# Moved load requests, an ACT copy, and re-timed weight splits and decode steps in a fused attention, MoE and gated-MLP kernel

## The chip, the cores and the metric

One Trainium2 chip, of which the kernel uses one core. The metric is the device time of one execution in microseconds (us), the median of several; lower is better.

## What is computed

The reference, cut to its three stages:

```python
# attention over pooled keys: q,k,v (8, 8, 576, 64); k and v are averaged over 8 neighbours -> 72
scores = q @ k_p.T / sqrt(64)
x = softmax(scores) @ v_p                  # -> x: 4608 tokens x 512
# MoE, top-1 of 8 experts
e = argmax(x @ w_gate); g = softmax(x @ w_gate)[e]
y = g * (relu(x @ w1[e]) @ w2[e])          # w1 (8, 512, 1024), w2 (8, 1024, 512)
# gated MLP, float64 weights
yn = y / sqrt(mean(y*y) + 1e-6) * rms_g
out = (silu(yn @ wg) * (yn @ wv)) @ w_out  # 512 -> 1536 -> 512
```

## The kernel before, in words

The program is one function, `fused`, written out in the order in which each engine gets its work. Float32 matmuls of the MoE and MLP are made of three fp32r ones: every operand is split into a rounded part `h` (a cast on ACT) and a rest `l` (a subtraction).

**Attention** (about 0 to 235 us) goes over 36 token tiles, n = 0 to 35 (loop at the end of the function's first half). A tile has an `emit_pt` (TensorE (PE) transposes of the probabilities), `emit_exp`, `emit_qt` for tile n+3, `emit_sc` (scores) for n+2, `emit_av` for n and `store` of the rows into `x_d` in DRAM. Between these lie five places "a" to "e"; `plan(n, place, f)` hangs a step on one, `run` issues what hangs there. So places are only positions in each engine's program: nothing runs before its operands are there, and an engine works its own list strictly in order. Nine tiles make two batches; the last of nine (tile 8, 17, 26, 35) is mixed and needs a zeroed block `qz` (L365, memset on POOL).

**Loads.** Ahead of the loop the requests for batches 0 and 1 are written out by hand for the SP queue (L763 to L779): `load_k`, `load_q(b, g, j)` (heads' half g, tokens' half j), `load_rows` (v) and `load_ends` (the last 64 key rows of several batches, eight requests of 48 KB). `sum_ends` on POOL adds those, `end_k` puts them into `kbd`, which the scores of that batch read. Requests share eight completion counters in turn, so a request is not issued before the one eight places ahead of it has landed.

**Routing.** `route_steps` gives for a group of tiles r1 (DVE: which expert), r3 (PE and DVE: rank inside the expert) and r4 (POOL: indirect stores of the token number to `ord_d`). After tile 18 `choose` to `choose_5` pick the expert for the first slots from what is known by then; `choose_2` writes the expert's number for SP (`first_expert`) and the places for `first_tokens`; `first_rows` gathers the rows of slot 0 into `xg` (L673), copies its logits to `lg0` (L676), and `xpose(0, c)` (in tiles 32 and 33) turns them on PE.

**First expert weights.** `load_w(i)` (tiles 25 to 28) brings eight blocks of 512 KB into `st`; `split_w(i, half)` makes `h` on ACT (L147, reported at the helper's line) and `l` on POOL (L148). Blocks 0 to 3 are w1, 4 to 7 w2.

**MoE slots** (about 235 to 700 us). `body(s)` works 256 tokens of one expert: eight `stage1(s, f)` (12 matmuls into one of four PSUM tiles `p`; relu `hh` on ACT, rest `hl` on DVE, which frees the tile), then `xpose` of the next slot, then `stage2` for one or two halves of 128 tokens. If the next slot has another expert ("fresh"), `change` and `change_half` split its weights beside this: w2 behind f = 3, the first half of w1 behind f = 4, the second behind f = 7, casts on ACT and four subtractions each on DVE.

**Decode steps.** In the same slots, `unit_steps(s, j)` turns float64 MLP weights into `uh` and `ul`, in two halves j = 0, 1 of five steps: s1 a square on ACT (writes `ub`), s2 two DVE instructions (write `ua`), s3 two (read `ub`, write `uh` and `ua`), s4 two (write `ub`), s5 one (reads `ub` and `ua`, writes `ul`). `ua` and `ub` are single buffers. Each step hangs on a place of `body`: 0 to 7 behind `stage1` f, 8 behind the next slot's `xpose` and w1 split, 9 behind the first half of `stage2`, 10 behind the second. `unit_load` brings the float64 data.

**MLP** (about 700 us to the end) has no part in the change.

Of the kernel before, what the change touches and what calls it, by code (L numbers as in the profile page):

```python
# [22 lines left out]
DM = 512  # L23
# [10 lines left out]
XW = DM + E  # L34
CUT = 18
SECOND = 30
EB = ((0,), (1, 2, 3), (4, 5, 6, 7))
# [12 lines left out]

R3 = [13, 17]

CW = [19, 30, 36, 46, 35, 52]

PLAIN = (0, 1, 2, 3, 4, 5)

# [25 lines left out]
def fused(ctx: ExitStack, tc: tile.TileContext, q, k, v, moe_w_gate, moe_w1, moe_w2,  # L82
          w_gate, w_val, w_out, rms_g, cst, out):
    nc = tc.nc
# [37 lines left out]
    lg0 = const.tile([128, 2, E], F32, name="lg0")  # L122
# [47 lines left out]
    def split_w(i, half, fresh=False):  # L170
        if fresh:
            for w, nm in ((w1h, "w1h"), (w1l, "w1l")) if i < 4 else ((w2h, "w2h"), (w2l, "w2l")):
                w[i % 4] = wtile(F32R, f"{nm}{i % 4}")
        hi, lo = (w1h[i], w1l[i]) if i < 4 else (w2h[i - 4], w2l[i - 4])
        c = slice(512 * half, 512 * half + 512)
        split(hi[:, c], lo[:, c], st[i][:, c], nc.gpsimd)
# [26 lines left out]
    def load_k(b):  # L203
        t = kq.setdefault(("k", b), [])
        for h4 in range(2):
            x = wtile(F32, f"k{h4}")
            nc.sync.dma_start(
                out=x.rearrange("p (h n) -> p h n", h=4),
                in_=k[b, 4 * h4:4 * h4 + 4, 0:512, :].rearrange("h (p r) d -> p h (r d)", r=4),
            )  # L210
            t.append(x)

    def load_q(b, g, j=None):
        t = kq["q", b] if ("q", b) in kq else kq.setdefault(("q", b), {})
        if g not in t:
            t[g] = wtile(F32, f"q{g}")
        c = slice(0, 256) if j is None else slice(128 * j, 128 * j + 128)
        nc.sync.dma_start(
            out=t[g].rearrange("p (h n) -> p h n", h=4)[:, :, c],
            in_=q[b, 4 * g:4 * g + 4, 0:512, :].rearrange("h (p r) d -> p h (r d)", r=4)[:, :, c])  # L220
# [10 lines left out]
    def load_ends(bs, eng=None):  # L231

        x = wtile(F32, "ke")
        n = len(bs)
        for h in range(H):
            (eng or nc.sync).dma_start(
                out=x[16 * h:16 * h + 16, 0:256 * n].rearrange("p (b n) -> p b n", b=n),
                in_=k[bs[0]:bs[-1] + 1, h, 512:576, :].rearrange("b (p r) d -> p b (r d)", r=4))
        kq["ke", bs] = x
# [26 lines left out]
    def load_rows(src, b, nm, hs=(0, 1, 2, 3)):  # L266
        t = kq.setdefault((nm, b), [])
        for h in hs:
            x = wtile(F32, f"{nm}{h}")
            nc.sync.dma_start(  # L270
                out=x[0:NP].rearrange("p (h n) -> p h n", h=2),
                in_=src[b, 2 * h:2 * h + 2].rearrange("h (p r) d -> p h (r d)", r=8))
            t.append(x)
# [321 lines left out]
    def xpose(s, c):  # L595

        px_ = px(c)
        for d in range(2):
            for z in range(2):
                nc.tensor.transpose(px_[:, d, 128 * z:128 * z + 128],  # L600
                                    xg[s][:, z, (2 * c + d) * 128:(2 * c + d) * 128 + 128], ident)
        hi, lo = (x[:, 2 * c:2 * c + 2] for x in xts[s])
        nc.scalar.copy(out=hi, in_=px_)
        nc.vector.tensor_tensor(out=lo, in0=px_, in1=hi, op=ALU.subtract)
        if c and s:
            gate_of(s)


    ev, xg, first = {}, {}, {}
# [60 lines left out]
    def first_rows():  # L670
        xg[0] = x_p.tile([128, 2, XW], F32, tag="xg0", bufs=1, name="xg0")
        for z in range(2):
            nc.gpsimd.indirect_dma_start(  # L673
                out=xg[0][:, z], out_offset=None, in_=x_d[0:CUT * 128, :],
                in_offset=bass.IndirectOffsetOnAxis(ap=tok0[:, z:z + 1], axis=0))
        nc.gpsimd.tensor_copy(out=lg0, in_=xg[0][:, :, DM:XW])  # L676
        xts[0] = tuple(wtile(F32R, "xt0").rearrange("p (c t) -> p c t", c=4) for _ in range(2))

    def second_tokens():
# [16 lines left out]
    def plan(n, where, f):  # L696
        at.setdefault((n, where), []).append(f)
# [42 lines left out]
        plan(CUT + i // 5, "abcde"[i % 5], f)  # L740
    for i in range(8):
        plan(CUT + 7 + i // 2, "ac"[i % 2], lambda i=i: load_w(i, ev[0], True))
        plan(CUT + 9 + (i + 1) // 2, "ca"[i % 2], lambda i=i: split_w(i, 0, True))
        plan(CUT + 9 + (i + 1) // 2, "eb"[i % 2], lambda i=i: split_w(i, 1))
    plan(CUT + 4, "e", choose_2)
    plan(CUT + 7, "e", choose_3)
    plan(CUT + 8, "e", choose_4)
    plan(CUT + 9, "e", choose_5)
    plan(SECOND - 2, "a", second_tokens)
    plan(SECOND, "c", second_rows)  # L750
    plan(NTL - 4, "b", lambda: xpose(0, 1))
# [19 lines left out]
    nc.sync.dma_start(out=wgl, in_=moe_w_gate.rearrange("(k p) e -> p k e", p=128))  # L771
    load_q(0, 1, 0)
    load_q(0, 0, 1)
    load_k(1)
    load_q(0, 1, 1)
    load_ends(EB[1])
    load_q(1, 0)
    load_rows(v, 1, "v")
    load_q(1, 1)  # L779
    nc.vector.memset(wg, 0.0)  # L780
    for t in vau:
# [171 lines left out]
    def unit_load(u, j):  # L953
        src, kk = unit_src(u, j)
        t = us_p.tile([128, 2 * DM + 2], I32 if wide else F32, tag="us", name="us")[:, 0:1024 if wide else 512]
        nc.sync.dma_start(out=t.rearrange("p (k n) -> p k n", k=kk), in_=src)
        ust[u, j] = t
# [41 lines left out]
    def unit_store(u):  # L999
        if stored(u):  # L1000
            for i, x in enumerate(held.pop(u)):
                nc.sync.dma_start(out=scr[u - EARLY, i], in_=x.bitcast(F32))
# [195 lines left out]
    late = []  # L1198
    for s in range(SURE):
        fill = {}  # L1200

        def put_in(place, f):
            fill.setdefault(place, []).append(f)

        if s == 0:
            for place, fs in tail.items():
                for f in fs:
                    put_in(place, f)
        if s == 1:
            put_in(0, lambda: gather(2))  # L1210
            put_in((1, 2), lambda: xpose(2, 0))
            put_in((1, 3), lambda: xpose(2, 1))
        for place, f in late:
            put_in(place, f)
        a = unit_steps(s, 0)
        b_ = unit_steps(s, 1)
        for place, f in zip((1, 2, 3, 5, 6) if s else [(0, 4)] * 5, a):
            put_in(place, f)
        if s + 1 < NU:
            put_in(7 if s else (0, 6), lambda s=s: unit_load(s + 1, 0))  # L1220
        else:
            put_in(7, ready)
            put_in(9, norm_0)
        for place, f in zip((7, 8, 8, 9) if s else [10] * 4, b_):
            put_in(place, f)
        late = [(0, b_[4]), (2, lambda s=s: unit_store(s))]
        if s + 1 < NU:
            late.append((1, lambda s=s: unit_load(s + 1, 1)))
        body(s, fill, 0 if s else 3)
        if s == 0:  # L1230
            sctx.close()
            vctx.close()
            psm = mctx.enter_context(tc.tile_pool(name="ps_m", bufs=1, space=PSUM))
            p1[:] = [psm.tile([128, T], F32, name=f"p1_{i}") for i in range(4)]
# [187 lines left out]
```

## Time and profile before

| | |
|---|---|
| median of 3 runs | 1651.44 us (1649.84 to 1652.1) |
| the profiled execution | 1655.93 us, of it span 1654.1 us |
| PE busy | 97% of the span, 9397 matmuls |
| DVE, ACT, POOL busy | 51%, 30%, 16% |
| granted TensorE clock, mean | 0.986 |
| DMA | 161.95 MB, mean 98 GB/s |

The span is cut into stages by what runs in them. For each the view of waits tells which engine was late, the timeline tells with what, and the granted clock tells the rest: 1.00 is 2.4 GHz, 0.50 is 1.2 GHz. Engine names: PE TensorE, DVE VectorE, ACT ScalarE, POOL GpSimd, SP the queue that issues DMAs. A line number is that of the kernel before; a helper's line stands for all its callers.

### The profile page before, as it was taken

To read this page: it belongs to the slowest core of one execution; us is meant where nothing else is said; L and a number is where in the kernel's file an instruction comes from. 1 tells how busy PE (TensorE), PEld (TensorE's weight loads), DVE (VectorE), ACT (ScalarE), POOL (GpSimd) and SP (SyncE) were. 2 spreads that over 40 slices of the span, in tenths; PEclk is the share of its full clock that TensorE was granted. 3 is DMA by queue.
4 is the path that set the end of the run, shared out by engine and by line. 5 is a ranking of instruction groups with operands and counts; after the bars stand their busy time and mean duration, and the time that the engine had idled before them with its cause. 6 is when DMAs were issued, how large, how long until landed. Compare 5 with 4: busy or idle time off the path is not lost. (4 is left out here: it accounts for less than half of the span.)

```text
span 1654.1 us, 26653 instructions
## 1 busy us (share of the span) xinstructions
PE 1596.7 (97%) x9397; PEld 1379.4 (83%) x9399; DVE 841.8 (51%) x1805; ACT 497.9 (30%) x1027; POOL 264.1 (16%) x363
## 2 busy tenths in 40 slices
PE   8999979989999989999999999999999999999997
PEld 6898868878888888998888888888888888888886
DVE  5688866688767686324443433333443333443222
ACT  3455623454434353322212112121221212122121
POOL 4687471110111011103000000000000000000000
PEclk9899989999999999999999999999999999999999
DMA  8977736476746463217400100010010001000000
GB/s 223 252 179 167 194 80 210 135 260 211 252 143 232 145 236 111 66 47 270 108 14 20 33 13 26 13 39 14 13 36 16 27 13 32 20 0 26 0 26 13
DMA packets 123515, 161.95 MB, mean 98 GB/s; under 512 B 36560, under 2 KB 85072, under 8 KB 123360
## 3 DMA queue, kind: packets, MB, share of 16 engines
q1 hardware_dynamic: 111328, 124.00, 26.4%
q0 software_dynamic: 11776, 35.91, 7.0%
q8 instruction: 77, 1.26, 0.3%
q14 instruction: 78, 0.64, 0.1%
q10 hardware_dynamic: 256, 0.13, 0.0%
HBM read 116.93 MB, written 43.08 MB: 97 GB/s over the span
## 5 line engine op out<-in xcount | busy, mean ns | idle before, releaser
L1319 DVE SCALAR_TENSOR_TENSOR th<-th,g 128x512 f32<-128x512 f32 (+1 forms) x120 | 76.1, 634 | 470.2 <-ACT th L1318 470.2
L1316 PE MATMUL g<-xh,rl 128*128 128x512 f32 (+1 forms) x576 | 217.5, 378 | 0.0
L1315 PE MATMUL g<-xl,rh 128*128 128x512 f32 (+1 forms) x576 | 217.5, 378 | 0.0
L1314 PE MATMUL g<-xh,rh 128*128 128x512 f32 (+1 forms) x576 | 217.5, 378 | 0.0
L1318 ACT ACTIVATE th<-g 128x512 f32<-128x512 f32 (+1 forms) x120 | 66.6, 555 | 461.8 <-PE g L1316 461.8
L1345 POOL DMA_INDIRECT out_dram<-o,tk x36 | 34.6, 962 | 815.7 <-ACT o L1344 788.6
L1340 PE MATMUL po<-rl,a 128*128 128x512 f32 x360 | 140.5, 390 | 1.5 <-DMA rl<-scr 1.5
L1339 PE MATMUL po<-rh,a 128*128 128x512 f32 x360 | 140.3, 390 | 0.0
L1341 PE MATMUL po<-rh,a 128*128 128x512 f32 x360 | 140.2, 389 | 0.0
L1315 PEld LDWEIGHTS g<-xl,rh 128*128 128x128 f32 x576 | 108.4, 188 | 20.2
L1314 PEld LDWEIGHTS g<-xh,rh 128*128 128x128 f32 x576 | 108.4, 188 | 20.2
L1316 PEld LDWEIGHTS g<-xh,rl 128*128 128x128 f32 x576 | 108.4, 188 | 19.9
L569 PE MATMUL p<-xh,w1h 128*128 128x256 f32 x672 | 110.9, 287 | 13.4 <-DVE hl L572 10.3
L147 ACT CAST a<-th 128x512 fp32r<-128x512 f32 (+1 forms) x120 | 69.3, 578 | 167.2 <-DVE th L1320 167.2
L148 DVE TENSOR_TENSOR a<-th,a 128x512 fp32r<-128x512 f32 (+1 forms) x120 | 76.7, 639 | 77.2 <-ACT a L147 77.2
L1314 PE MATMUL g<-xh,uh 128*128 128x512 f32 (+1 forms) x288 | 108.9, 378 | 1.7 <-DVE th L1320 1.7
L569 PEld LDWEIGHTS p<-xh,w1h 128*128 128x128 f32 x672 | 94.0, 192 | 19.0 <-DVE hl L572 11.1
L1316 PE MATMUL g<-xh,ul 128*128 128x512 f32 (+1 forms) x288 | 108.8, 378 | 0.0
L1315 PE MATMUL g<-xl,uh 128*128 128x512 f32 (+1 forms) x288 | 108.7, 378 | 0.0
L569 PE MATMUL p<-xl,w1h 128*128 128x256 f32 x672 | 108.7, 285 | 0.0
L569 PE MATMUL p<-xh,w1l 128*128 128x256 f32 x672 | 108.0, 283 | 0.0
L572 DVE SCALAR_TENSOR_TENSOR hl<-p,hh 128x256 fp32r<-128x256 f32 x168 | 70.6, 421 | 62.5 <-ACT hh L571 56.4
(307 smaller groups left out, 3013.8 us busy)
## 6 DMA issues: line engine op xcount, KB each, us to landing
st<-in_moe_w_dram SPq DMA_DIRECT2D x64, 512.0 KB
y_d<-ys SPq DMA_DIRECT2D x39, 257.0 KB
v<-in_v_dram SPq DMA_DIRECT2D x32, 288.0 KB
y<-y_d SPq DMA_DIRECT2D x68, 128.0 KB
x_d<-x SPq DMA_DIRECT2D x16, 520.0 KB
k<-in_k_dram SPq DMA_DIRECT2D x16, 512.0 KB
q<-in_q_dram SPq DMA_DIRECT2D x14, 512.0 KB
scr<-uh SPq DMA_DIRECT2D x13, 512.0 KB
```

Source lines behind the costliest of these rows:

```text
L147: nc.scalar.copy(out=hi, in_=src)
L148: eng.tensor_tensor(out=lo, in0=src, in1=hi, op=ALU.subtract)
L569: nc.tensor.matmul(a, lhsT=w[d][:, fs], rhs=x[:, d], start=j + d == 0, stop=j == 2 and d == 3)
L572: nc.vector.scalar_tensor_tensor(out=lo, in0=a, scalar=0.0, in1=hi, op0=ALU.max, op1=ALU.subtract)
L1314: nc.tensor.matmul(g[:, j], lhsT=wh[:, sl], rhs=hi[:, d], start=d == 0, stop=False)
L1315: nc.tensor.matmul(g[:, j], lhsT=wh[:, sl], rhs=lo[:, d], start=False, stop=False)
L1316: nc.tensor.matmul(g[:, j], lhsT=wl[:, sl], rhs=hi[:, d], start=False, stop=d == 3)
L1318: nc.scalar.activation(out=th, in_=g[:, 0], func=AF.Tanh, scale=0.5)
L1319: nc.vector.scalar_tensor_tensor(out=th, in0=th, scalar=1.0, in1=g[:, 0], op0=ALU.add, op1=ALU.mult)
L1339: nc.tensor.matmul(po, lhsT=a[:, 0, tsl], rhs=wh[:, sl], start=c == 0, stop=False)
L1340: nc.tensor.matmul(po, lhsT=a[:, 0, tsl], rhs=wl[:, sl], start=False, stop=False)
L1341: nc.tensor.matmul(po, lhsT=a[:, 1, tsl], rhs=wh[:, sl], start=False, stop=c == NC2 - 1)
```

## The change

1. SP's first requests: `load_q(0, 1, 1)` is issued ahead of `load_k(1)`, and `load_ends(EB[1])` (batches 1 to 3) behind v of batch 1.
2. The copy of slot 0's logits to `lg0` leaves POOL, where it stood right behind the gather, and is done by ACT in `xpose(0, 1)`, the first of slot 0 (tile 32).
3. The eight `split_w` pairs are hung on places given by a table, both halves of a block together; `choose_2` moves from tile 22 e to 23 d, `choose_5` from 27 e to 28 a.
4. Decode steps and `unit_load` get other places in `body`; the last step of half 1 is no longer carried over into the next slot.

```diff
@@ -50,7 +50,9 @@
 
 R3 = [13, 17]
 
-CW = [19, 30, 36, 46, 35, 52]
+CW = [19, 30, 36, 46, 35]
+
+SPLIT = [(27, "a"), (27, "c"), (28, "a"), (28, "c"), (30, "c"), (31, "a"), (32, "a"), (32, "c")]
 
 PLAIN = (0, 1, 2, 3, 4, 5)
 
@@ -599,6 +601,8 @@
             for z in range(2):
                 nc.tensor.transpose(px_[:, d, 128 * z:128 * z + 128],
                                     xg[s][:, z, (2 * c + d) * 128:(2 * c + d) * 128 + 128], ident)
+        if c and not s:
+            nc.scalar.copy(out=lg0, in_=xg[0][:, :, DM:XW])
         hi, lo = (x[:, 2 * c:2 * c + 2] for x in xts[s])
         nc.scalar.copy(out=hi, in_=px_)
         nc.vector.tensor_tensor(out=lo, in0=px_, in1=hi, op=ALU.subtract)
@@ -673,7 +677,6 @@
             nc.gpsimd.indirect_dma_start(
                 out=xg[0][:, z], out_offset=None, in_=x_d[0:CUT * 128, :],
                 in_offset=bass.IndirectOffsetOnAxis(ap=tok0[:, z:z + 1], axis=0))
-        nc.gpsimd.tensor_copy(out=lg0, in_=xg[0][:, :, DM:XW])
         xts[0] = tuple(wtile(F32R, "xt0").rearrange("p (c t) -> p c t", c=4) for _ in range(2))
 
     def second_tokens():
@@ -740,12 +743,13 @@
         plan(CUT + i // 5, "abcde"[i % 5], f)
     for i in range(8):
         plan(CUT + 7 + i // 2, "ac"[i % 2], lambda i=i: load_w(i, ev[0], True))
-        plan(CUT + 9 + (i + 1) // 2, "ca"[i % 2], lambda i=i: split_w(i, 0, True))
-        plan(CUT + 9 + (i + 1) // 2, "eb"[i % 2], lambda i=i: split_w(i, 1))
-    plan(CUT + 4, "e", choose_2)
+        n, w = SPLIT[i]
+        plan(n, w, lambda i=i: split_w(i, 0, True))
+        plan(n, w, lambda i=i: split_w(i, 1))
+    plan(CUT + 5, "d", choose_2)
     plan(CUT + 7, "e", choose_3)
     plan(CUT + 8, "e", choose_4)
-    plan(CUT + 9, "e", choose_5)
+    plan(CUT + 10, "a", choose_5)
     plan(SECOND - 2, "a", second_tokens)
     plan(SECOND, "c", second_rows)
     plan(NTL - 4, "b", lambda: xpose(0, 1))
@@ -771,11 +775,11 @@
     nc.sync.dma_start(out=wgl, in_=moe_w_gate.rearrange("(k p) e -> p k e", p=128))
     load_q(0, 1, 0)
     load_q(0, 0, 1)
+    load_q(0, 1, 1)
     load_k(1)
-    load_q(0, 1, 1)
-    load_ends(EB[1])
     load_q(1, 0)
     load_rows(v, 1, "v")
+    load_ends(EB[1])
     load_q(1, 1)
     nc.vector.memset(wg, 0.0)
     for t in vau:
@@ -1214,16 +1218,16 @@
             put_in(place, f)
         a = unit_steps(s, 0)
         b_ = unit_steps(s, 1)
-        for place, f in zip((1, 2, 3, 5, 6) if s else [(0, 4)] * 5, a):
+        for place, f in zip((0, 0, 1, 2, 7) if s else [(0, 4)] * 5, a):
             put_in(place, f)
         if s + 1 < NU:
-            put_in(7 if s else (0, 6), lambda s=s: unit_load(s + 1, 0))
+            put_in(4 if s else (0, 6), lambda s=s: unit_load(s + 1, 0))
         else:
             put_in(7, ready)
             put_in(9, norm_0)
-        for place, f in zip((7, 8, 8, 9) if s else [10] * 4, b_):
+        for place, f in zip((7, 7, 9, 9, 10) if s else [10] * 5, b_):
             put_in(place, f)
-        late = [(0, b_[4]), (2, lambda s=s: unit_store(s))]
+        late = [(2, lambda s=s: unit_store(s))]
         if s + 1 < NU:
             late.append((1, lambda s=s: unit_load(s + 1, 1)))
         body(s, fill, 0 if s else 3)
```

Lines of the changed kernel are 2 to 4 later than the same lines before.

**SP, the requests ahead of the loop** (`ke` is `load_ends`, `q_190` tokens of batch 0 in heads' half 1, `q_207` or `q_198` and `q_217` batch 1). Before:

```order
L218 DMA q_190<-in_q_dram 128x4x128
L218 DMA q_169<-in_q_dram 128x4x128
L207 DMA k_193<-in_k_dram 128x4x256
L207 DMA k_195<-in_k_dram 128x4x256
L218 DMA q_190<-in_q_dram 128x4x128
L236 DMA ke<-in_k_dram 16x3x256 x8
L218 DMA q_207<-in_q_dram 128x4x256
L270 DMA v_209<-in_v_dram 72x2x512
L270 DMA v_211<-in_v_dram 72x2x512
L270 DMA v_213<-in_v_dram 72x2x512
L270 DMA v_215<-in_v_dram 72x2x512
L218 DMA q_217<-in_q_dram 128x4x256
```

With the change:

```order
L220 DMA q_190<-in_q_dram 128x4x128
L220 DMA q_169<-in_q_dram 128x4x128
L220 DMA q_190<-in_q_dram 128x4x128
L209 DMA k_194<-in_k_dram 128x4x256
L209 DMA k_196<-in_k_dram 128x4x256
L220 DMA q_198<-in_q_dram 128x4x256
L272 DMA v_200<-in_v_dram 72x2x512
L272 DMA v_202<-in_v_dram 72x2x512
L272 DMA v_204<-in_v_dram 72x2x512
L272 DMA v_206<-in_v_dram 72x2x512
L238 DMA ke<-in_k_dram 16x3x256 x8
L220 DMA q_217<-in_q_dram 128x4x256
```

The second `q_190` now stands ahead of the two k requests, and the eight `ke` go from in front of batch 1's first q to in front of its second one.

**POOL, tiles 27 to 30** (`w1l`, `w2l` are the splits' rests, `lg` the logits, `ord_d` the store of r4). Before:

```order
L673 DMA xg_2465<-x_d,tok_88 128x520 x2
L676 COPY lg_91<-xg_2465 128x16
L148 TENSOR_TENSOR w1l_2489<-st_2293,w1h_2488 128x512 x2
L148 TENSOR_TENSOR w1l_2536<-st_2342,w1h_2535 128x512 x2
L148 TENSOR_TENSOR w1l_2571<-st_2367,w1h_2570 128x512 x2
L148 TENSOR_TENSOR w1l_2608<-st_2409,w1h_2607 128x512 x2
L148 TENSOR_TENSOR w2l_2643<-st_2439,w2h_2642 128x512 x2
L148 TENSOR_TENSOR w2l_2689<-st_2492,w2h_2688 128x512 x2
L365 MEMSET qz 64x512 x2
L552 DMA ord_d<-tok,rpi 36864x1
```

With the change:

```order
L150 TENSOR_TENSOR w1l_2440<-st_2293,w1h_2439 128x512 x2
L677 DMA xg_2471<-x_d,tok_88 128x520 x2
L150 TENSOR_TENSOR w1l_2494<-st_2342,w1h_2493 128x512 x2
L150 TENSOR_TENSOR w1l_2536<-st_2367,w1h_2535 128x512 x2
L150 TENSOR_TENSOR w1l_2576<-st_2409,w1h_2575 128x512 x2
L367 MEMSET qz 64x512 x2
L554 DMA ord_d<-tok,rpi 36864x1
```

The copy is gone, one split stands ahead of the gather, and the memset of `qz` has four split pairs ahead of it in place of six.

**DVE, a slot's start up to its w2 split, in one slot of the middle** (the steps in it: s5 writes `ul`, s2 `ua`, s3 `uh` and `ua`, s4 `ub`). Before:

```order
L572 SCALAR_TENSOR_TENSOR hl<-p_0_3393,hh 128x256
L994 SCALAR_TENSOR_TENSOR ul_3693<-ub,ua 128x512
L572 SCALAR_TENSOR_TENSOR hl<-p_1_3394,hh 128x256
L572 SCALAR_TENSOR_TENSOR hl<-p_2_3395,hh 128x256
L978 TENSOR_SCALAR ua<-us 128x512
L980 SCALAR_TENSOR_TENSOR ua<-us,ua 128x512
L572 SCALAR_TENSOR_TENSOR hl<-p_3_3396,hh 128x256
L1015 TENSOR_LOAD row_i
L1028 COMPARE_AND_BRANCH
L1028 UNCONDITIONAL_BRANCH
L148 TENSOR_TENSOR w2l_2643<-st_3373,w2h_2642 128x1024
```

With the change:

```order
L998 SCALAR_TENSOR_TENSOR ul_3694<-ub,ua 128x512
L574 SCALAR_TENSOR_TENSOR hl<-p_0_3394,hh 128x256
L982 TENSOR_SCALAR ua<-us 128x512
L984 SCALAR_TENSOR_TENSOR ua<-us,ua 128x512
L574 SCALAR_TENSOR_TENSOR hl<-p_1_3395,hh 128x256
L988 SCALAR_TENSOR_TENSOR uh_4073<-ub,ua 128x512
L990 TENSOR_SCALAR ua<-uh_4073 128x512
L574 SCALAR_TENSOR_TENSOR hl<-p_2_3396,hh 128x256
L993 TENSOR_SCALAR ub<-us 128x512
L994 SCALAR_TENSOR_TENSOR ub<-us,ub 128x512
L574 SCALAR_TENSOR_TENSOR hl<-p_3_3397,hh 128x256
L1019 TENSOR_LOAD row_i
```

s3 and s4 of half 0 have moved ahead of the w2 split, and s5 of half 1 ahead of the slot's first `hl`.

## Rows read from the trace of the kernel before

**Rows 1.** The page's first part: busy us (share of the span) and instructions.

```profile
PE 1596.7 (97%) x9397; PEld 1379.4 (83%) x9399; DVE 841.8 (51%) x1805; ACT 497.9 (30%) x1027; POOL 264.1 (16%) x363
```

**Rows 2.** What PE waited for, whole span: us in total, times, longest.

```profile
PE p L569 <- DVE hl L572: 10.3, 4, 3.3
PE sc L403 <- POOL qz L365: 6.8, 1, 6.8
PE pq L376 <- DMA q<-in_q_dram: 3.9, 4, 1.6
...
PE y L1050 <- DVE hl L572: 3.4, 7, 0.9
...
PE av L447 <- DVE rmx L503: 2.5, 1, 2.5
PE sc L403 <- DVE rs L451: 2.0, 1, 2.0
```

**Rows 3.** Windows: us, engines' busy time (instructions), then PEclk, DMA share, GB/s.

```profile
22.00:25.00 3.00, 2.88 (x31) 2.63 (x32) 1.23 (x3) 0.83 (x2) 0.18 (x1) 1.00 0.25 33
36.00:48.00 12.00, 11.42 (x73) 10.21 (x72) 5.06 (x8) 3.02 (x7) 5.33 (x8) 0.57 1.01 263
210.00:231.00 21.00, 15.30 (x132) 14.36 (x133) 12.17 (x36) 3.84 (x10) 18.77 (x26) 0.77 0.16 48
515.00:525.00 10.00, 8.18 (x57) 7.97 (x56) 9.07 (x15) 5.94 (x10) 0.74 (x2) 0.83 0.87 296
```

**Rows 4.** Timeline of SP, 14 to 26 us: start, us, queue, line, transfer.

```profile
15.01 7.31 SPq L236 DMA_DIRECT2D ke<-in_k_dram  x8
22.36 1.27 SPq L218 DMA_DIRECT2D q<-in_q_dram  x1
...
25.74 0.40 SPq L218 DMA_DIRECT2D q<-in_q_dram  x1
```

**Rows 5.** Timeline of PE, 35 to 36 us: start, us, work, [idle before <-releaser].

```profile
35.74 0.52 PE L376 MATMUL pq<-cc,q 128*128 128x128 f32 x3 [1.55 <-DMA q<-in_q_dram]
```

**Rows 6.** Timeline of POOL, 183 to 224 us.

```profile
183.04 0.96 POOL L673 DMA_INDIRECT xg<-x_d,tok  x1 [0.30 <-issue]
197.55 0.19 POOL L676 COPY lg<-xg 128x16 f32<-128x16 f32 x1 [13.55 <-DMA xg<-x_d,tok]
197.72 9.87 POOL L148 TENSOR_TENSOR w1l<-st,w1h 128x512 fp32r<-128x512 f32 x8
...
212.53 1.10 POOL L365 MEMSET qz<- 64x512 f32 x2
...
219.87 3.76 POOL L148 TENSOR_TENSOR w2l<-st,w2h 128x512 fp32r<-128x512 f32 x3
```

**Rows 7.** Timeline of PE, 203 to 214 us.

```profile
203.04 0.66 PE L600 MATMUL px<-cc,xg 128*128 128x128 f32 x4
...
213.11 2.52 PE L403 MATMUL sc<-kbd,qz 128*64 128x72 f32 x32 [6.82 <-POOL qz L365]
```

**Rows 8.** Timeline of DVE: end of `choose_2`, and r3's cast in two tiles.

```profile
161.81 1.07 DVE L635 SCALAR_TENSOR_TENSOR ev_i<-m 1x1 int32<-1x1 f32 x1
...
193.63 0.17 DVE L531 CAST rpi<-rpf 128x5 int32<-128x5 f32 x1
...
220.12 3.53 DVE L531 CAST rpi<-rpf 128x4 int32<-128x4 f32 x1
```

**Rows 9.** Timeline of DVE, one fresh slot and the next one's start, 337 to 354 us.

```profile
337.00 0.68 DVE L984 SCALAR_TENSOR_TENSOR uh<-ub,ua 128x512 fp32r<-128x512 f32 x1
...
347.48 2.56 DVE L148 TENSOR_TENSOR w1l<-st,w1h 128x512 fp32r<-128x512 f32 x4 [0.54 <-ACT w1h L147]
...
353.50 0.42 DVE L572 SCALAR_TENSOR_TENSOR hl<-p,hh 128x256 fp32r<-128x256 f32 x1
```

**Rows 10.** What ACT waited for longest, 260 to 700 us.

```profile
ACT ub L975 <- DVE ul L994: 67.1, 25, 5.5
```

**Rows 11.** Timeline of PE at the same slot's start, 352 to 355 us.

```profile
353.98 0.83 PE L569 MATMUL p<-xh,w1h 128*128 128x256 f32 x4 [3.23 <-DVE hl L572]
```

## Prediction

> **What bounds the kernel now.** The page's first part comes first: TensorE is busy 97% of the span [rows 1], so no other engine's total matters. A change can win only where TensorE stands idle, or where it works at half clock. The view of TensorE's waits therefore comes next [rows 2]. The largest ones are 10.3 us for `hl` ahead of `stage1`, 6.8 us once for `qz`, 3.9 us for four q loads, 3.4 us for `hl` ahead of `stage2`, 2.5 us for `rmx` and 2.0 us for `rs`. The third view is the granted clock by windows [rows 3]: 0.57 in 36 to 48 us, 0.77 in 210 to 231, 0.83 in 515 to 525, where 1.00 is 2.4 GHz and 0.50 is 1.2 GHz. Each of these stretches holds or follows one of the waits. What a wait can give is its own length and, in such a place, the half clock's cost; I count the latter as (1 - granted clock) x window, less the idle time in it. The change touches only these waits, so the sum goes over them. It is made against the profiled execution, 1655.93 us, which is 4.5 us over the median of the runs, 1651.44; the same difference is then taken from the median.
>
> **Part 1, requests.** With eight completion counters, q of batch 1 cannot be issued before the first of eight `ke` has landed: the `ke` are issued from 15.01 to 22.3 us and q follows at 22.36, its second part at 25.74 [rows 4]. Between 22 and 25 us the DMA share is only 0.25 [rows 3], so 3.0 x 0.75 = 2.25 us of transfer time is lost. TensorE meets this at 35.74, idle 1.55 us for q, one of the four waits of 3.9 us together [rows 2, 5]. With the change, q and v of batch 1 are asked for ahead of the `ke`, and the hole closes: **-2.3 us**. Bounds: 0, if the hole comes back behind v, since the second q now stands directly behind the eight `ke`; +2.3, if `sum_ends` and `end_k` of batch 1 get the `ke` so late that the scores wait as long as q did; and -7.5, if the half clock of 36 to 48 us goes too (0.43 x 12 = 5.2). Its window moves with the start, and I see no reason why it should vanish, so it stays. The q of batch 0 asked for earlier only moves k of batch 1 back by one request, which has the same later gate; at nothing.
>
> **Part 2, the tiles before the slots.** POOL shows one chain [rows 6]. It issues the gather at 183.04, then the copy of the logits stands idle 13.55 us for the landing, at 197.55. Only then do eight halves of w1's split run (9.87 us), four of w2's, and at 212.53 the memset of `qz`. TensorE's scores wait for that 6.82 us, to 213.11 [rows 7]. The next product waits 2.5 us for `rmx` [rows 2]: the last three w2 splits run on POOL from 219.87 for 3.76 us, and the cast at 220.12 on DVE takes 3.53 us where the same cast took 0.17 at 193.63 [rows 6, 8]. The two ended together, so I read it as one held by the other.
>
> With the change, nothing on POOL waits for the gather. The `qz` memset has four pairs of splits ahead of it, and the loads of those are there at their tiles; 9.9 us of work from about 183 us on, with some 2 us for the gather's issue between, end near 195. That is 11 us ahead of the need (213.11 - 6.82 = 206.3), so **-6.8**. The `rmx` wait goes if tile 33's r3 no longer meets a split: the last one is now at tile 32 c; **-2.5**. In 210 to 231 us the clock was low after these idle stretches: 0.23 x 21 = 4.8 less about 1.0 of idle that the window's average may hold, **-3.8**. `choose_2`, the last of whose instructions ended at 162.88 on DVE [rows 8], stood ahead of a tile's softmax, and TensorE waited 2.0 for `rs` [rows 2]; one tile later and behind the softmax, **-2.0**.
>
> New costs. ScalarE now has four casts of a tile's split in tiles 27, 28 and 32 in a row, ahead of `ptsb` or `vbd`; and r3 and r1 of tiles 27 to 31 can now meet a split on POOL. Such a meeting costs DVE up to 3.53 - 0.17 = 3.36 us [rows 8], and TensorE what exceeds its slack. From below it is 0 (DVE is no bound at 51%); from above 5.4 (one full meeting and 2.0 of late `ptsb`, the size of the `rs` wait). I take **+2.0**, nearer the lower end, because the splits that held the cast for 3.53 us were three in a row, and now at most two stand together in these tiles. Part 2 in all: -6.8 - 2.5 - 3.8 - 2.0 + 2.0 = **-13.1**.
>
> At nothing: the logits' copy on ScalarE (0.19 us on POOL [rows 6]; ScalarE is at 30%). The gather's issue is later by one pair of splits, 2 x 1.23 = 2.5 us; it landed at 197.55 and its first reader on TensorE stood at 203.04 [rows 6, 7], so 3 us of cover are left; were it gone, each us late is a us lost. `choose_2` a tile later delays the places for `first_tokens` and SP's read of the expert's number, whose weights come to be split from tile 27 on; POOL has its stores of tile 26 to do until then. `choose_5` feeds slots that start after 235 us.
>
> **Part 3, the slots.** In a fresh slot DVE is late at the start of the slot. The steps of the decode work, 0.68 us for a 128x512 instruction, and four w1 subtractions, 2.56 us, stand ahead of `hl` [rows 9], and TensorE, with its four tiles full, stands 3.23 us [rows 11]. Besides, ScalarE waited 25 times, 67.1 us in all and 5.5 at most, for `ul` ahead of the square [rows 10], with the casts of the next x behind it. With the change s3 and s4 lie ahead of the w2 split, and between the w1 split and `hl` stands s3 to s5 of half 1 in place of s2 to s4: one instruction less, some 0.4 us. The square of half 1 no longer stands behind the late s5 of half 0, so that the casts of x come earlier; by 0 to 2.7 us (67.1/25), of which I take 1.6. `hl` is then 2.0 us earlier at each site. Of the four waits of 10.3 us [rows 2] the long ones, 3.3 and 3.2, lose 2.0 each, and the other two, 10.3 - 3.3 - 3.2 = 3.8, go wholly: -7.8. Of the 3.4 us ahead of `stage2` I count half, as the rest lies ahead of the same sites: -1.7. With 515 to 525 us back at 1.00, 0.17 x 10 = -1.7. Part 3: **-11.2**. Bounds: -2 or so, if the work only changes places (rival 1); all of 10.3 + 3.4 + 1.7 = -15.4, if hl is early by more than 3.3. `unit_load` three places earlier waits on SP alone, behind w2's loads, whole groups ahead of its use; at nothing.
>
> **The sum:** -2.3 - 13.1 - 11.2 = -26.6; 1655.93 - 26.6 = 1629.3 for the profiled execution, 1651.44 - 26.6 = about **1625 us** as a median.
>
> **The rivals.**
> 1. *The slots' work only moves.* DVE has the same instructions in a slot, and the w1 split stays ahead of `hl`; s3 and s4, moved ahead, delay the w2 split and with it w1's. Then only some 2 us of part 3 come: -2.3 - 13.1 - 2 = -17.4, 1634. For it: 841.8 us of DVE work stay [rows 1]. Against: the waits are short, and 2 us end two of them.
> 2. *Splits and DVE collide.* The change does not do what it says of the tiles: POOL, no longer held back, runs the splits beside r1 and r3 of tiles 27 to 33. Two meetings of 3.36 us instead of the 2.0 counted, and the 2.5 of `rmx` back in another tile: +6 to +7, 1632. For it: the cast's 3.53 against 0.17 [rows 8]. Against: the rows show no wait of TensorE on r3 other than that one. The Trainium skill (GPSIMD Engine Reference, Key points) says that GpSimd shares its SBUF interfaces with VectorE and contends with DVE instructions in a two-port mode or with two SBUF inputs; by that rule, r1's products of two SBUF operands collide as well as the cast, and the time would be this rival's. The trace agrees for the cast alone.
> 3. *Slower.* Step s1 of half 0 is now at place 0 of ScalarE, right behind the first `hh`, and its `ub` is free only when s5 of the slot before is through on DVE, behind a w1 split of 2.56 us [rows 9]. Behind it queue the next three `hh`, which `hl` and so the PSUM tiles need. It decides where ScalarE's wait exceeds the cover of the four tiles. The 67.1 us that ScalarE waited for just this [rows 10] cost TensorE little; if 2 us pass through in each of the 17 slots behind the first (the kernel has 18 units of decode work), that is +34: -26.6 + 34 = +7.4, 1659. For it: the waits were up to 5.5 us. Against: s5 now stands ahead of the slot's first `hl`.
> 4. *Better.* Both remaining low clocks go (-5.2) and part 3 comes in full (-4.2): -36, 1615.
>
> **Chances.** Forecast 0.58, rival 1 0.18, rival 2 0.12, better 0.07, slower 0.05. The range: the good ends, -7.5, -13.1 - 2.0 (no new costs) and -15.4, give -38, 1613; the poor ends, +2.3, -13.1 + 3.4 (the new costs at 5.4) and -2, give -9.4, 1642. That leaves out rival 3 and some tails. A measurement can tell 0.2%, 3.3 us, from no change: only rival 3 comes near that, so faster 0.94, same 0.02, slower 0.04.
>
> **What would show it.** In the profile after: q's waits near 1.5 us in all; no idle of 13 us on POOL; no wait for `qz` or `rmx`; a granted clock of 1.00 from 200 to 230; `hl` ahead of `stage1` at 2.5 and not 10.3; ScalarE's wait for `ul` much shorter. The prediction is wrong if `hl` waits keep their sum, if new waits on `ptsb`, `vbd`, `hh` or `rs` of over 3 us stand in tiles 27 to 34 or at places 0 and 1, or if xg is what ends the wait at 203.

## The result, and the profile after

The changed kernel takes 1630.58 us (median of 4 runs, 1627.53 to 1637.83), the kernel before, on the same chip, 1651.36 us. The medians differ by 20.8 us. Two more runs of the changed kernel took 1635.05 and 1632.16 us; over all six the ratio of the means is 0.9886, with a 95% interval of 0.9859 to 0.9912, which is 18.9 us: faster. The forecast was 1625, the range 1613 to 1642. The profiled execution of the changed kernel is the slowest of the four, 1637.83 us; against the profiled one of before, 1655.93, it is 18.1 us shorter, and the sum of the prediction, -26.6, is held against these 18.1.

The page's first part, after. No engine's total has moved much, as in [rows 1]; TensorE (PE) does the same 9397 matmuls in 7 us less, some 5 of them because less time passes at half clock: the mean granted clock goes from 0.986 of 1654.1 us to 0.989 of 1636.0.

```profile
PE 1589.5 (97%) x9397; PEld 1375.5 (84%) x9399; DVE 840.1 (51%) x1805; ACT 498.0 (30%) x1028; POOL 264.0 (16%) x362
```

TensorE's waits over the span, after (us in total, times, longest), to be read beside [rows 2]:

```profile
PE p L571 <- DVE hl L574: 8.4, 5, 3.0
...
PE pq L378 <- DMA q<-in_q_dram: 3.0, 2, 2.7
PE sc L399 <- DVE rs L453: 2.1, 2, 1.9
PE av L446 <- DVE x L477: 1.9, 3, 1.0
...
PE p L571 <- ACT xh L607: 1.0, 1, 1.0
```

The waits for `qz` (6.8) and `rmx` (2.5) are gone, and so is the 3.4 for `hl` ahead of `stage2`. The wait for `hl` ahead of `stage1` has fallen by 1.9 only, the one for q by 0.9, and `rs` stands again with 1.9, now in another place. The windows, after (us, busy time of PE, PEld, DVE, ACT, POOL, then granted clock, DMA share, GB/s):

```profile
22.00:25.00 3.00, 3.00 (x35) 2.90 (x34) 1.93 (x4) 0.64 (x2) 0.99 (x2) 1.00 0.83 176
35.00:47.00 12.00, 11.42 (x76) 10.25 (x74) 5.30 (x8) 3.02 (x7) 9.06 (x14) 0.57 0.98 265
200.00:221.00 21.00, 19.91 (x201) 18.75 (x201) 17.84 (x54) 11.59 (x27) 16.89 (x23) 0.93 0.23 77
346.00:350.00 4.00, 4.00 (x23) 4.00 (x22) 3.93 (x8) 3.81 (x5) 0.00 (x0) 0.57 0.79 259
500.00:510.00 10.00, 10.00 (x88) 10.00 (x87) 9.68 (x20) 7.32 (x14) 0.96 (x1) 1.00 0.92 295
```

Against [rows 3]: the DMA hole of 22 to 25 us is closed, 0.25 to 0.83; the half clock at 35 us is as it was, 0.57; the stretch that was at 0.77 is at 0.93, and the one at 0.83 is at 1.00. The half clock of 346 to 350 us follows a wait for `hl` that stayed.

Where the 18.1 us lie is read from the start of the same matmuls in both. First the timeline of PE before:

```profile
152.11 0.69 PE L339 MATMUL pvg<-wg,vt 128*72 128x64 f32 x8 [0.58 <-DVE slot L621]
...
166.16 1.73 PE L444 MATMUL av<-both,ptsb 96*128 96x146 f32 x12 [0.38 <-DVE x L475]
...
252.82 0.28 PE L929 MATMUL op__3353<-cc,ogf 32*128 32x32 f32 x2 [0.81 <-DVE ogf L925]
```

and PE after, with px to be held against 203.04 in [rows 7]:

```profile
150.87 0.69 PE L341 MATMUL pvg<-wg,vt 128*72 128x64 f32 x8 [0.57 <-DVE slot L625]
...
162.94 1.73 PE L446 MATMUL av<-both,ptsb 96*128 96x146 f32 x12 [0.37 <-DVE x L477]
...
203.98 0.66 PE L602 MATMUL px<-cc,xg 128*128 128x128 f32 x4
...
242.37 0.28 PE L933 MATMUL op__3353<-cc,ogf 32*128 32x32 f32 x2 [0.84 <-DVE ogf L929]
```

| stretch | predicted | measured, each the difference of two such gains | the same from e5's profile |
|---|---|---|---|
| part 1, to 152 us | -2.3 | 152.11 - 150.87: -1.2 | -2.9 |
| `choose_2`, to 166 us | -2.0 | 3.2 - 1.2: -2.0 | -2.0 |
| tiles to `px` | +2.0, all of the new costs | 203.98 - 203.04 = 0.9 later, so +4.2 | +4.2 |
| `px` to 252 us | -13.1 (`qz`, `rmx`, clock) | 10.4 earlier, so -11.4 | -10.3 |
| slots, to the end | -11.2 | 18.1 - 10.4: -7.7 | -12.5 |

The last column is the same kernel, profiled in e5 on another chip at 1632.52 us, against the same profile of before (its starts are 149.24, 161.30, 202.41 and 241.93). The rows for `choose_2` and the tiles to `px` agree to 0.1 us, the one behind them to 1.1. Part 1 and the slots differ by 1.7 and 4.8 us between the two profiles, so their sizes are known no better than that.

### The profile page after: what moved, and what is told of

Its sections match the earlier page's. It is cut to its first block, busy times and chain, and to the rows that moved or that the text cites. A ratio compares the mean times of both kernels' runs of the same rounds, so it can differ in the third digit from the quotient of the medians.

```text
span 1636.0 us, 26656 instructions
## 1 busy us (share of the span) xinstructions
PE 1589.5 (97%) x9397; PEld 1375.5 (84%) x9399; DVE 840.1 (51%) x1805; ACT 498.0 (30%) x1028; POOL 264.0 (16%) x362
```

## The experiments

The groups of runs were on different chips, and the kernel before took 1661.0 us beside e1 to e4, 1649.9 beside e5 to e8, 1648.3 beside e9 to e11 and 1665.4 beside e12. So each kernel is compared by its ratio to the kernel before of its own group, with the 95% interval in brackets.

### e1 to e3: each part alone, in the kernel before

```diff
 load_q(0, 0, 1)
+load_q(0, 1, 1)
 load_k(1)
-load_q(0, 1, 1)
-load_ends(EB[1])
 load_q(1, 0)
 load_rows(v, 1, "v")
+load_ends(EB[1])
 load_q(1, 1)
```

> Only part 1 (the order of SP's first requests) in the kernel before. Theory: the wait for q is not removed but gathered: q loads cost TensorE 2.7 us once in place of 3.7 us in three, so -1.2 us at 150 us into the span and at the end, within 0.2% of before. Rival: the hole closes as predicted, -2.3 us or more, and the half clock of 36 to 47 us gets shorter.

0.9996 [0.9975, 1.0018]: no gain that can be told. The interval is some 3.6 us to either side, so the time does not decide between the theory's -1.2 and the prediction's -2.3. In the trace the wait for q is as the theory has it, at 35.08 us and 2.70 in one piece. Why shows in the changed kernel's own timeline of SP (start, us, transfer):

```profile
17.81 12.73 SPq L238 DMA_DIRECT2D ke<-in_k_dram  x8
30.58 0.43 SPq L220 DMA_DIRECT2D q<-in_q_dram  x1
```

Behind v the eight `ke` take 12.73 us to issue in place of 7.31 [rows 4], and the last q goes out at 30.58, not at 25.74. The hole is closed and the wait has moved behind it. In e1's profile the granted clock is 0.72 over 35 to 47 us, which the rival would have as a gain; but it is 0.72 in e2 too, where the requests stand as before, so it is not of this edit.

```diff
+        if c and not s:
+            nc.scalar.copy(out=lg0, in_=xg[0][:, :, DM:XW])
-        nc.gpsimd.tensor_copy(out=lg0, in_=xg[0][:, :, DM:XW])
...
+        n, w = SPLIT[i]
+        plan(n, w, lambda i=i: split_w(i, 0, True))
+        plan(n, w, lambda i=i: split_w(i, 1))
-    plan(CUT + 4, "e", choose_2)
+    plan(CUT + 5, "d", choose_2)
...
```

> Only part 2 (logits' copy on ScalarE, table of splits, choose_2 and choose_5) in the kernel before. Theory: the qz wait of 6.8, the rmx wait of 2.5 and one rs wait of 2.0 go, and new waits of some 3.5 us come in tiles 28 to 32, where DVE's roh and rpi of r1 and r3 are held by splits on POOL (2 to 2.7 us for 0.2); net -9 us, with parts 1 and 3 as before. Rival: the new waits come from ScalarE's casts ahead of ptsb; then ptsb or vbd is named as releaser and DVE's rows stay at 0.2.

0.9944 [0.9924, 0.9965], 9.3 us by the ratio. The `qz` wait does not occur. That DVE is held shows once, at 209.20 us, where `roh` takes 1.71 us; at 185.45 and 199.78 us `roh` and the cast take 0.20 and 0.17. The new waits are thus not those of the theory: the longest is 2.1 us for `vbd`, which the rival names, but ScalarE itself stood idle 2.22 us ahead of that `vbd`, so no cast held it.

```diff
-        for place, f in zip((1, 2, 3, 5, 6) if s else [(0, 4)] * 5, a):
+        for place, f in zip((0, 0, 1, 2, 7) if s else [(0, 4)] * 5, a):
-        for place, f in zip((7, 8, 8, 9) if s else [10] * 4, b_):
+        for place, f in zip((7, 7, 9, 9, 10) if s else [10] * 5, b_):
-        late = [(0, b_[4]), (2, lambda s=s: unit_store(s))]
+        late = [(2, lambda s=s: unit_store(s))]
...
```

(`unit_load` of half 0 moves from place 7 to 4 with them.)

> Only part 3 (places of the decode steps and of unit_load) in the kernel before. Theory: waits for hl ahead of stage2 go (3.4 to 0), those ahead of stage1 fall from 10.3 to about 8, since half 1's s3 to s5 stand in one piece between the w1 split and the first hl; -5 to -8 us in all with the clock. Rival 1: work only moves, -2 us or less. Rival 2: the square at place 0 blocks ScalarE, slower than before.

0.9926 [0.9906, 0.9946], 12.3 us by the ratio and 11.2 between the medians, more than expected. In its profile the waits are as the theory says: 7.1 us in 4 for `hl` ahead of `stage1`, none on the list ahead of `stage2`. The surplus over 8 us is not explained; its profiled execution is the slowest of its four, so the trace does not hold it. The three ratios together give 0.04 + 0.56 + 0.74 = 1.34%, the whole change, on other chips, 1.14% (1.08% in e5): the parts add up within their intervals.

### e4 and e10: the request for the last q

```diff
     load_rows(v, 1, "v")
-    load_ends(EB[1])
     load_q(1, 1)
+    load_ends(EB[1])
```

> The changed kernel with the second q of batch 1 asked for ahead of the eight requests for the last key rows, not behind them. Theory: the wait of 2.7 us for q at 34.7 us goes to 1 us or less, and nothing waits for the key rows; -2 us against the changed kernel, and up to -7 if the half clock of 35 to 46 us goes with the idle time ahead of it. Rival: the wait moves to end_k, whose kbd the next scores read, and the time stays within 1 us.

0.9919 [0.9903, 0.9936], no better than the changed kernel (0.9892 in e5, on another chip). The rival holds. PE in e4:

```profile
32.34 0.63 PE L378 MATMUL pq<-cc,q 128*128 128x128 f32 x4 [0.39 <-DMA q<-in_q_dram]
...
36.08 0.48 PE L334 MATMUL pe__508<-cc,es 128*64 128x64 f32 x4 [3.12 <-POOL es L248]
```

q is 0.39 late, and the sum of the last key rows, which now come last, is 3.12 late.

```diff
     load_rows(v, 1, "v")
-    load_ends(EB[1])
     load_q(1, 1)
...
     end_k(0)
+    load_ends(EB[1], nc.scalar)
```

> The changed kernel with the eight requests for the last key rows issued by ScalarE's queue at 13 us, so that they stand neither ahead of q nor behind it in SP's queue. Theory (the wait of 2.7 us for q at 34.7 us is made by the place of eight small requests in one queue with eight counters): q at most 1 us late and es not late either, -2 to -3 us, up to -7 if the half clock of 35 to 44 us goes. Rival: it is the bandwidth of the first 35 us that is short, or ScalarE is held up by its own counters; then q, es or pe come as late as before.

0.9992 [0.9979, 1.0004]: most of the gain is lost. The second rival holds, and more than it said; the wait for q is gone from the list, as the theory had it. ACT in e10:

```profile
18.83 0.33 ACTq L238 DMA_DIRECT2D ke<-in_k_dram  x1
25.57 7.43 ACTq L238 DMA_DIRECT2D ke<-in_k_dram  x7
33.05 0.68 ACT L416 ACTIVATE pe<-pe 128x576 f32<-128x576 f32 x1 [19.97 <-DMA ke<-in_k_dram]
```

ScalarE, which issues the requests itself, stands 20 us, and PE's next scores 17.36 us with it. SP could afford to stand; ScalarE could not.

### e5 and e8: the changed kernel again, and choose_2 put back

> The changed kernel itself, as the measure for the three that run with it and for the second q's variant before. Theory: 1.0 to 1.3% below the kernel before. Rival: on a chip on which the experts' weights land later the gain is smaller, since ScalarE's casts in tiles 27 and 28 then stand longer ahead of vt, vbd and ptsb.

1633.33 us, 0.9892 [0.9862, 0.9923], the same as the first measurement. Its longest waits are those of the first profile, too (`hl` 7.1, q 2.8, `rs` 2.1), so they are no accident of one execution.

```diff
-    plan(CUT + 5, "d", choose_2)
+    plan(CUT + 4, "e", choose_2)
```

> The changed kernel with choose_2 where it was, in tile 22 e. Theory: one wait for rs of 2.0 us at 165 us comes back, +2 us. Rival: an earlier choose_2 also asks for the weights earlier by some us, and where they land late this gives the 2 us back: same time or faster.

0.9901 [0.9865, 0.9937], 1633.40 beside 1633.33 us. The wait of 1.97 for `rs` at 161.39 us is back, and the time is not longer. The rival held as to the time, but not by its reason, since the first weights are asked for only 0.9 us earlier than in e5 (163.50 beside 164.44 us) and the last 1.0 us later (180.52 beside 179.49). What differs is in the tiles: `roh`, the cast and the second `roh` take 0.66, 0.37 and 0.19 us in e8, and 2.74, 2.01 and 2.24 in e5. So `px` stands 2.8 us earlier in e8 (199.63 beside 202.41), and the slots lose that again (`hl` ahead of `stage1` 9.6 us in place of 7.1); why they do was not tested. On the three steps see e6.

### e6, e9 and e12: what holds DVE in tiles 27 to 33

In the changed kernel, POOL's splits (first fence) run beside DVE's rank steps (second):

```profile
181.14 2.50 POOL L150 TENSOR_TENSOR w1l<-st,w1h 128x512 fp32r<-128x512 f32 x2
...
186.08 7.41 POOL L150 TENSOR_TENSOR w1l<-st,w1h 128x512 fp32r<-128x512 f32 x6
193.55 1.10 POOL L367 MEMSET qz<- 64x512 f32 x2
...
202.46 2.50 POOL L150 TENSOR_TENSOR w2l<-st,w2h 128x512 fp32r<-128x512 f32 x2
```

```profile
181.07 2.64 DVE L508 TENSOR_TENSOR roh<-lgs,rmx 128x40 f32<-128x40 f32 x1
...
191.51 2.02 DVE L533 CAST rpi<-rpf 128x5 int32<-128x5 f32 x1
...
202.36 2.65 DVE L508 TENSOR_TENSOR roh<-lgs,rmx 128x32 f32<-128x32 f32 x1
```

Each of the three ends with the split beside it. PE then waits, each time a few microseconds later:

```profile
188.11 1.73 PE L446 MATMUL av<-vbd,ptsb 96*128 96x146 f32 x12 [0.53 <-DVE x L477]
...
196.89 1.15 PE L399 MATMUL sc<-kbd,qt 64*128 64x108 f32 x16 [1.90 <-DVE rs L453]
...
209.55 1.73 PE L446 MATMUL av<-vbd,ptsb 96*128 96x146 f32 x12 [0.96 <-DVE x L477]
```

```diff
-SPLIT = [(27, "a"), (27, "c"), (28, "a"), (28, "c"), (30, "c"), (31, "a"), (32, "a"), (32, "c")]
+SPLIT = [(27, "e"), (28, "a"), (28, "c"), (29, "e"), (30, "c"), (31, "e"), (32, "a"), (32, "c")]
```

> The changed kernel with three split pairs behind the rank steps of their tile: places 27 e, 29 e and 31 e for 27 a, 28 c's successor and 31 a. Theory (DVE's roh and rpi are held while a split runs on POOL): DVE's roh at the end of tiles 27 and 31 and its cast in tile 29 take 0.2 us again in place of 2.0 to 2.7, TensorE's waits for rs and x of 0.5, 1.9 and 1.0 us go, -3 us or more against the changed kernel. Rival: those waits come from ScalarE's casts; then they stay though DVE's instructions are short, and the time stays.

0.9890 [0.9853, 0.9928]: no gain. `roh` is short in both tiles and the wait of 0.53 us behind the first is gone, but the cast in tile 29 is held longer, since now eight subtractions stand in a row on POOL (9.86 us from 181.42). DVE and PE in e6:

```profile
187.90 3.42 DVE L533 CAST rpi<-rpf 128x5 int32<-128x5 f32 x1
```

```profile
194.68 2.05 PE L399 MATMUL sc<-kbd,qt 64*128 64x108 f32 x16 [3.31 <-DVE rs L453]
```

With e8 this makes a series: the cast takes 2.02, 3.42 and 0.37 us (in e8, at 190.47), and PE waits 1.90, 3.31 and not at all for `rs` behind it. So the wait is the cast's time less 0.1 us in the two long cases and none in the short one, while ScalarE's casts ahead of `ptsb` cost 0.45 to 0.57. Of the wait of 0.96 at 209.55 us this is not so: in e6 `roh` of tile 31 is short, and 0.78 of that wait stays.

```diff
-            mx = sm_p.tile([128, n, 1], F32, tag="rmx", name="rmx")
+            r_ = ps.tile([128, n, E + 1], F32, tag="pp", name="roh")
+            mx = r_[:, :, E:E + 1]
-            oh = sm1.tile([128, n, E], F32, tag="roh", name="roh")
+            oh = r_[:, :, 0:E]
-            pf = sm_p.tile([128, n], F32, tag="rpf", name="rpf")
+            pf = rk[:, 0, 0:n]
```

> The changed kernel with the small arrays of r1 and r3 in PSUM (rmx, roh, rpf), so that DVE's roh and the cast of rpf no longer read two operands or one wide one from SBUF. Theory (they are held because they share a way into SBUF with POOL's splits): roh and the cast take 0.2 to 0.4 us even while a split runs, and TensorE's waits for rs (1.9) and x (0.5, 1.0) in tiles 28 to 33 go with the half clock of 197 to 200 us: -3 to -5 us against the changed kernel. Rival: they are held by something else (the memory of lgs, or the order of semaphores), stay at 2 us and more, and the time stays.

1.0059 [1.0036, 1.0083], slower than before, but the question is answered. POOL and DVE in e9:

```profile
200.60 2.49 POOL L150 TENSOR_TENSOR w1l<-st,w1h 128x512 fp32r<-128x512 f32 x2
...
234.40 2.51 POOL L150 TENSOR_TENSOR w2l<-st,w2h 128x512 fp32r<-128x512 f32 x2
```

```profile
202.65 0.20 DVE L509 TENSOR_TENSOR roh<-lgs,roh 128x40 f32<-128x40 f32 x1
...
234.79 0.16 DVE L534 CAST rpi<-rk 128x4 int32<-128x4 f32 x1
...
235.38 1.56 DVE L540 TENSOR_SCALAR rpi<-rpi 128x4 int32<-128x4 int32 x1
```

The first two lie inside a split and take what they take alone; `roh` has one input and its output in PSUM, the cast its input. The third, beside the same split as the cast and with all its operands in SBUF, is held to the split's end and takes 1.56 us, where it takes 0.17 alone. So it was the operands in SBUF. The loss is a new one: the only tile of that PSUM tag is now DVE's for the whole of r1 and r3, and PE waits for it six times (`pv`, `ptv`, `pvg`, `pe__887`: 4.9 + 2.5 + 2.5 + 2.5 + 1.7 us, and half clocks behind them).

> Both edits together on the changed kernel. Theory: they lie in different stretches and add up, -5 to -8 us against the changed kernel, some 1.4 to 1.6% below the kernel before.

1.0131 [1.0108, 1.0155]: with e9's and e10's edits the losses nearly add. Over the changed kernel's 0.9892 they are 1.7% and 1.0% alone and 2.4% together.

```diff
-SPLIT = [(27, "a"), (27, "c"), (28, "a"), (28, "c"), (30, "c"), (31, "a"), (32, "a"), (32, "c")]
+SPLIT = [(27, "e"), (28, "a"), (28, "c"), (29, "e"), (30, "c"), (31, "e"), (32, "a"), (32, "c")]
-            pf = sm_p.tile([128, n], F32, tag="rpf", name="rpf")
+            pf = rk[:, 0, 0:n] if n1 == 27 else sm_p.tile([128, n], F32, tag="rpf", name="rpf")
```

> The table of e6 (splits at 27 e, 29 e and 31 e) with the rpf of the rank step in tile 29 in the PSUM tile of rk, which nothing else wants in tiles 29 to 31. Theory: the one DVE instruction that a split still held there, the cast (3.4 us), takes 0.2 us, TensorE's wait for rs of 3.3 us and the half clock of 193 to 200 us go, and no wait for PSUM comes in its place: -3 to -6 us against the changed kernel, 1.4% below the kernel before. Rival: the cast is short and the next wait in line (ptsb, or x at 207 us) takes the time, less than 2 us in all.

0.9893 [0.9873, 0.9912], like the changed kernel. The cast takes 0.17 us and no wait for `rs` follows, but this run does not decide: the splits ran later on that chip and none was beside the cast (203.54 us; a split to 202.07, then the memset). Whether the version gains where the splits run early stays open.

### e7: the steps behind the first hl

```diff
-        for place, f in zip((0, 0, 1, 2, 7) if s else [(0, 4)] * 5, a):
+        for place, f in zip((3, 5, 5, 6, 7) if s else [(0, 4)] * 5, a):
-        for place, f in zip((7, 7, 9, 9, 10) if s else [10] * 5, b_):
+        for place, f in zip((7, 7) if s else [10] * 5, b_):
-        late = [(2, lambda s=s: unit_store(s))]
+        late = ([(0, b_[2]), (1, b_[3]), (2, b_[4])] if s else []) + [(2, lambda s=s: unit_store(s))]
```

(The load of the next unit's second half moves to place 2 with them.)

> The changed kernel with the last three steps of half 1 behind the next slot's hl 0, 1 and 2 and half 0's steps behind the w2 and w1 splits. Theory: the waits for hl ahead of stage1 (8.4 us) come from the 2.9 us of s3 to s5 between the w1 split and the first hl; they fall to 3 us or less, -5 us, and with the half clock behind them up to -9. Rival: the capacity of DVE in a half slot is what is short, and the waits come back behind the w2 or w1 split, as y or p on hl; same time or slower.

0.9928 [0.9902, 0.9954], 1638.98 beside 1633.33 us: the rival holds. The waits in e7:

```profile
PE y L1054 <- DVE hl L574: 7.2, 8, 2.0
...
PE p L571 <- ACT xh L607: 3.5, 3, 1.3
```

The wait ahead of `stage1` has left the head of the list, and as much stands ahead of `stage2` and for the next slot's x. What moves is the place of the wait. In the changed kernel DVE is busy for 14.2 of the 15.4 us from 329.2 to 344.6 us, up to the long wait for `hl`, so it is read as DVE time that is short in a slot with one half and fresh weights behind it. The edit moves the steps of both halves, and does not tell which move brought which wait.

## Why the prediction was right, and where its sum was not

**The bound** held: TensorE is at 97% before and after, and the time went where its waits and half clocks went.

**Part 1** was forecast at -2.3 and gave -1.2; TensorE's waits for q fell from 3.9 to 3.0 us. The hole was read rightly and closed; the step that failed is taking its 2.25 us as the gain. The lower bound, that the hole "comes back behind v", is half of what came: the last q is issued 4.8 us later than before. e4 showed the next in line, `es`, so that no order of these requests on SP tried here gives more. The half clock stayed in this profile (0.57); its length differs between executions: in e5 it is 0.72, and (0.72 - 0.57) x 12 = 1.8 us is about the 1.7 by which e5's part 1 is better.

**Part 2** was forecast at -13.1 and gave -2.0 + 4.2 - 11.4 = -9.2. Right were the 13.55 us of POOL [rows 6], the memset (ready at 194.65, needed at 207.36), `rmx` and `choose_2`'s wait. The failed step is the term "+2.0" for new costs: it measured 4.2, twice (e5). Rival 2 had the mechanism, and its price per meeting (up to 3.36): three meetings hold DVE for 2.64, 2.02 and 2.65 us. PE's part ahead of `px` is 0.53 + 1.90 of wait and about 1.7 of half clock (199.3 to 202.6 us), beside 0.45 for ScalarE's cast, and less the 1.0 us that TensorE before had lost in this stretch on `ptsb`, at 199.18 us; some 0.6 is unaccounted for. The wait of 0.96 us at 209.55 lies behind `px`, and e6 ties 0.2 of it at most to the third meeting. The reason given for the small value, that at most two splits stand together, was wrong: with nothing on POOL between the gather in tile 27 and the memset, six halves run in a row, and the order of POOL's work printed with the change has these three pairs one behind the other. The rule of the Trainium skill (GPSIMD Engine Reference, Key points), that GpSimd contends with a VectorE instruction with two SBUF inputs, holds for `roh`, here 2.64 us against 0.20 with one of its inputs and its output in PSUM. The prediction gave such meetings too little weight, and its reading that the trace agrees for the cast alone missed rows of DVE before:

```profile
159.38 1.50 DVE L513 TENSOR_TENSOR rob<-roh,rcm 128x32 bf16<-128x32 f32 x1
...
202.77 1.20 DVE L509 SCALAR_TENSOR_TENSOR roh<-roh,cc 128x32 f32<-128x32 f32 x1
```

Both have two inputs in SBUF and took some 0.2 us elsewhere, and POOL worked beside them, on sums of k and v and on the splits. So r1 did meet POOL before the change; the first of the two stands directly ahead of `choose_2`, and so of the 2.0 us that TensorE waited for `rs`.

And `choose_2`'s 2.0 us, though measured, bring nothing in the whole kernel (e8): up to `px` its move costs some 2.5 us more than it gives, since with it the rank steps meet the splits for longer, so the 4.2 is largely the price of these 2.0.

**Part 3** was forecast at -11.2 and gave -7.7 (-12.5 in e5's profile). Right were the waits ahead of `stage2` (3.4 to none on the list, forecast at half) and 500 to 510 us at full clock. Right, too, was "`hl` is then 2.0 us earlier at each site", when it is counted from the slot's first `px`. At the site of [rows 11] the wait went only from 3.23 to 2.71. PE and ACT there, before:

```profile
336.13 1.03 PE L600 MATMUL px<-cc,both 128*128 128x128 f32 x8
...
344.54 0.99 PE L569 MATMUL p<-xh,w1h 128*128 128x256 f32 x4 [0.33 <-ACT xh L603]
```

```profile
343.92 1.05 ACT L603 CAST xh<-px 128x512 fp32r<-128x512 f32 x2
```

PE, ACT and DVE there, after:

```profile
329.23 1.04 PE L602 MATMUL px<-cc,both 128*128 128x128 f32 x8
...
336.02 0.73 PE L571 MATMUL p<-xh,w1h 128*128 128x256 f32 x4
...
344.62 0.74 PE L571 MATMUL p<-xh,w1h 128*128 128x256 f32 x4 [2.71 <-DVE hl L574]
```

```profile
335.13 1.05 ACT L607 CAST xh<-px 128x512 fp32r<-128x512 f32 x2
```

```profile
338.70 2.56 DVE L150 TENSOR_TENSOR w1l<-st,w1h 128x512 fp32r<-128x512 f32 x4 [0.54 <-ACT w1h L149]
...
343.54 0.69 DVE L998 SCALAR_TENSOR_TENSOR ul<-ub,ua 128x512 fp32r<-128x512 f32 x1
344.14 0.42 DVE L574 SCALAR_TENSOR_TENSOR hl<-p,hh 128x256 fp32r<-128x256 f32 x1
```

From `px` to `hl` it is 14.9 us, before 353.50 - 336.13 = 17.4 [rows 9]: 2.5 earlier, and 1.4, 2.1 and 2.1 at the other three sites (near 389, 504 and 597 us after). Both causes named are there: from `px` to `xh` it is 5.9 us in place of 7.8, and from the split's start to `hl` 5.4 in place of 6.0. ACT's wait for `ul`, on which the first of them rested [rows 10], fell from 67.1 to 45.9. What failed is to take these 2.0 us off the wait: TensorE comes to it sooner, too, 6.8 us behind `px` in place of 8.4, since its waits of 0.49 and 0.43 us for `hl` ahead of `stage2` and of 0.33 for `xh` are gone. That is one gain on one path, and the sum has a part of it twice. From `px` to the fifth tile of `stage1` the four sites give 2.5 + 1.4 + 2.0 + 2.1 = 8.0 us, all waits ahead of it included.

The other step that failed is that part 3 has no term for new costs. In slot 1 TensorE waits for `xh` and `xl`, with a half clock from 271 us:

```profile
268.13 1.00 PE L571 MATMUL p<-xh,w1h 128*128 128x256 f32 x4 [0.95 <-ACT xh L607]
...
270.11 1.15 PE L571 MATMUL p<-xl,w1h 128*128 128x256 f32 x4 [0.51 <-DVE xl L608]
```

Before it waited 0.48 us for `xh` there and none for `xl`. From that slot's `px` to the fifth tile of `stage1` it is 14.2 us in place of 11.0, 3.2 lost (1.8 in e5); why `xh` and `xl` are later was not tested. And at 439.84 us a wait of 1.38 (0.67 in e5) is new, where ACT and DVE stood for data that came late from DMA: `unit_load`, which the prediction had at nothing. e7 says that no other place tried for the steps does better.

**The rivals.** Rival 1, with 2 us left of part 3, did not hold in that size: the four sites gave 8.0. Rival 2 held in its mechanism, at 2.2 us over what was counted in place of 6 to 7. Rival 3, ScalarE held at place 0 by `ul`, is seen, but small: the square at 344.26 us waits 2.33, at the same place where `hl` is late anyway. The median, 1630.58, is nearer to the 1632 and 1634 of rivals 2 and 1 than to 1625, so the number alone would not have told them apart; the rows above do. It came out inside the range although in these profiles all three parts fell short, by 1.1, 3.9 and 3.5 us: that room was in the range, not in the sum.

The signs to look for came out as follows: no idle of 13 us on POOL and no wait for `qz` or `rmx`, right; no wait for xg at `px`, right; ACT's wait for `ul` shorter, right (45.9); q at 1.5, wrong (3.0); clock of 1.00 from 200 to 230, nearly (0.93, in 200 to 221); `hl` at 2.5, wrong (8.4).

## What to carry to other kernels

A wait that goes is worth its length less what comes next in line: ask of each moved request, split and step what then stands last in its queue, and count that first. Two waits on one path are not two gains: when the first goes, the engine comes sooner to the second and stands there longer. An engine that is freed from a wait does its work in one piece and earlier; what runs beside it there, on an engine that shares operands' memory with it, is the price. Where an engine has too much to do in one stretch, changing the order moves the wait and does not end it.

## What the runs showed of the hardware

A DVE instruction of 0.2 us with its operands in SBUF took up to 3.53 us beside subtractions on POOL ([rows 8]; 3.42 in e6), over the ends of single ones of 1.23 us. With an input in PSUM two of them were not held at all (0.20 and 0.16 in e9), while one in SBUF beside the same split took 1.56.

In four of the five profiles from the chips on which the kernel before took 1661 and 1665 us (e1, e3, e4, e12), DVE, and in all but e3 ScalarE at the same time, stood still for 3.1 to 5.8 us between 180 and 191 us, while the first expert's weights were loading, and the trace names no instruction of the program as releaser. ACT, then DVE, in e4:

```profile
191.23 0.95 ACT L354 COPY vbd<-pv 96x438 f32<-96x438 f32 x2 [4.61 <-remote]
```

```profile
191.15 0.17 DVE L453 TENSOR_SCALAR rs<-av 128x8 f32<-128x8 f32 x1 [4.44 <-remote]
```

No profile from the chips of 1648 to 1651 us has such a wait. Its cause was not looked into, nor whether it is what makes those chips slower.
